# Sixteen block sums re-dealt between the token loop and the spatial mixing of layer one (seven and nine in place of six and ten)

## The chip, the core and the metric

The program runs on one core of one Trainium2 chip. The metric is the device time of one execution in microseconds (us): the median of three runs before the change is 1368.55 us, the runs lie between 1368.22 and 1369.3 us. Times inside the program are given in us from the start of the span of one profiled execution.

## The reference, cut to what is computed

Two layers follow each other, each a block A and a block B, all in float32, over a sequence of 2048 tokens of width 512. Both layers use the same weights.

```
x = x + A(layernorm(x)); x = x + B(layernorm(x))        # twice
A: qkv = x @ wqkv; linear attention of 32 heads of 16 (phi = elu + 1); @ wo
B: z = gelu(x @ w_in)                  # 2048 x 1792
   z1, z2 = halves of z; z2 = layernorm(z2)
   g = w_sp @ z2 + b_sp                # w_sp is 2048 x 2048: mixes tokens
   out = (z1 * g) @ w_out
```

The product `w_sp @ z2` is the spatial mixing. The change touches its preparation in layer one (L = 0 in the code).

## The kernel before

**Arithmetic.** Every operand of a matmul is split in two fp32r parts: a high part, rounded by ScalarE (ACT; `high`, L135, or L1457 and L1462 in the mixing), and a low part, the rest, subtracted by VectorE (DVE; `low`, L138, or L1466, L1470 and L1472). A product is then three matmuls: high by high, high by low, low by high. So TensorE (PE) is fed by a chain of load, high part, low part.

**Phases of one layer.** `P1` is the first half of A (projections and the state of the linear attention). `P2` is the loop over 16 blocks of 128 tokens that finishes A and makes z1 and z2; it runs steps s = 1 to 18 and is called the second half here. `P4` is the mixing with the output product behind it. In layer one its steps g = 0 to 47 are six products of eight steps each, in the order P4 (g 0 to 7), P1 (8 to 15), P6 (16 to 23), P7 (24 to 31), P5 (32 to 39), P3 (40 to 47), and then 14 steps of a nested product N2.

**Why there are sums.** The mixing is a 2 x 2 block product by Winograd's scheme: seven products in place of eight, of which some need sums of blocks of `w_sp` as an operand. `Sums` (L1174) makes them. One unit of it (`fetch`, `sum`, `store`) loads three 128 x 512 pieces of `w_sp` over the queue of SyncE (SP; L1195), makes three additions on GpSimd (POOL; L1209) and stores three pieces to DRAM as S1, S3 and S2 (L1202). There are 16 such units, in fixed order; number 2k + j belongs to step k of the products P6 (reads S2), P7 (S3) and P5 (S1). Sixteen more units follow, one addition and one store each, for S4 (product P3). They load a piece of S2 and one of `w_sp` (L131).

**What sets the order.** The program is recorded in the order of the Python code, and each engine and queue works through its own instructions in that order. Tables at the head of the file say at which step a unit is made:
- `TOKEN_TICKS` (L29): steps of the second half at which a unit is made. The first of its three pieces goes to the z tile of the same number, the two others to pages; the load is issued at the end of the step before. SP stores the result at the start of the next step.
- `MIX_TICKS` (L31): steps g of the mixing at which the remaining units are made, in `tick` (L1212): the load at step g - 1, the additions at step g and the stores behind them, issued by POOL.
- `MIX_UNITS` (L32): steps g at which a unit of the kept sums of N2 is made (`Inner.unit`, L1287): one addition on DVE (L1296 to L1306), a high part on ACT (L135) into a fresh page, and at the next step the low part on DVE (`finish`, L138). SP stores both (L1267). The loads of a unit (L1263) are issued two steps ahead of it.

**A step of the mixing.** `P4.run` (L1759) does for step g: `prepare(g + 2, g + 3)`, that is ACT L1457 and DVE L1466 for the weight of step g + 2, and DVE L1433, ACT L1462, DVE L1470 for the z operand of step g + 3; then the matmuls of step g (`acc`, L1619 to L1621); `fetch(g + 4)`, a load of S2 or S3 by SP (L1415), or of `w_sp` (L1413); `tick`; the unit of N2; and behind the last step of a product `evac` (L1649), in which DVE reads the six accumulating banks out (L1669 behind P6). P6 and P7 add to the same banks, so P7 can't begin in a bank that DVE has not read.

**Pages.** SBUF is dealt in 23 pages of 128 x 512 by `Slots` (L39): a page that was given back first is handed out first, and the new writer waits for the last reader or the last transfer of the page. A page behind a store is given back with a lag of six pages (`STORE`).

Of the kernel before, what the change touches and what calls it, by code (L numbers as in the profile page):

```python
# [25 lines left out]
PHI_EPS = 1e-6  # L26
DEFER = 6
STORE, POOL = 6, 3
TOKEN_TICKS = {at: (at,) for at in (5, 7, 9, 11, 12, 13)}  # L29
SPARE_TAGS = {14: 15, 16: 15}  # L30
MIX_TICKS = (2, 4, 5, 7, 8, 10, 12, 14, 16, 17, 20, 21, 23, 24, 26, 27, 29, 30, 32, 34, 35, 37, 38, 39, 40, 41)  # L31
MIX_UNITS = (10, 14, 20, 22, 25, 31, 36, 40), (1, 3, 5, 7, 9, 11, 13, 15)  # L32
MAKE_AT = 5, 7, 9
ROW_UNITS = range(1, 9)
INNER_UNITS = range(47, 55, 2)
# [55 lines left out]
def mixer_kernel(ctx: ExitStack, tc: tile.TileContext, x_in, wqkv, wo_d, win1_d, win2_d, wsp_d, bsp_d, wout_d,  # L91
# [680 lines left out]
    class P2:  # L772
# [308 lines left out]
        def run(self, sums):  # L1081
# [3 lines left out]
            for s in range(1, NT + 3):  # L1085
# [54 lines left out]
                if self.L == 0:  # L1140
                    sums.sum(s, TOKEN_TICKS)
                if s >= 15:
# [25 lines left out]
                self.xturn.load(s - 1)  # L1168
                if self.L == 0 and s + 1 in TOKEN_TICKS:
                    sums.fetch(TOKEN_TICKS[s + 1])  # L1170
            self.win2.free()
# [191 lines left out]
    class P4:  # L1363
# [395 lines left out]
        def run(self, nxt):  # L1759
# [3 lines left out]
            n = len(self.steps)  # L1763
            own, units = inner["N2" if self.nest_late else "N1"], MIX_UNITS[self.L]
            sums_at = {}
# [7 lines left out]
            for g in range(n):  # L1773
# [8 lines left out]
                if self.nest_late:  # L1782
                    self.sums.tick(g, MIX_TICKS)
                    if g == 34:
# [134 lines left out]
```

## Time and profile before

| | us |
|---|---|
| median of three runs | 1368.55 |
| the profiled execution's own time | 1368.05 |
| its span, first to last instruction | 1366.3 |
| PE busy in the span | 1354.5 |
| DVE, ACT, POOL busy | 1037.8, 638.4, 500.9 |
| PE idle in front of a matmul, all waits that the trace lists | 8.2 |
| second half of layer one, s = 1 to 18 | about 140 to 330 |
| mixing of layer one, g = 0 to 47 | 344.75 to 580 |

PE is busy almost throughout, so its few idle places, and the places where it runs slowly, are what the other engines can still give or take. A row of the timeline has the start, the duration, the engine, the line, what is written from what, how many instructions are merged in the row, and in brackets how long the engine sat idle before it and what released it. "pg" is a page, "qd" a tile of 128 x 2048, "bank" a bank of PSUM, "s" one of the sums in DRAM.

### The profile page before, as it was taken

Reading aid. Unit: us, or ns where it says so; the run is one execution under the profiler, and the core shown is the slowest. Engines: PE = TensorE matmul, PEld = TensorE weight load, DVE = VectorE, ACT = ScalarE, POOL = GpSimd, SP = SyncE. Lnnn points to the kernel's source line nnn. Section 1 sums busy time; section 2 is a strip of 40 time slices with the busy share of each in tenths; the row PEclk is TensorE's granted clock in tenths of the full one; section 3 lists DMA queues with packets and bytes.
Section 4 is the critical chain, followed back from the end, with each engine's and each line's share of the span. In section 5 each row is a group of like instructions: output and inputs, shape, how many; then the busy total and the mean of one; then the engine's idle time right before and its main releaser. Section 6 shows DMA issues by size and latency. Waiting matters only on the chain.

```text
span 1366.3 us, 18345 instructions
## 1 busy us (share of the span) xinstructions
PE 1354.5 (99%) x6087; PEld 1133.1 (83%) x6087; DVE 1037.8 (76%) x1582; ACT 638.4 (47%) x1021; POOL 500.9 (37%) x597
## 2 busy tenths in 40 slices
PE   9999999999999899999999999999999999999998
PEld 7888888888888688888888888888888888888887
DVE  7985898876867789976678768887767798978642
ACT  6875553446442333442456655444455534533310
POOL 2333475533377347426421133543230011412240
PEclk9999999999999999999999999999999999999999
DMA  5762388966798888895776534666568799569552
GB/s 182 240 210 88 123 262 257 301 229 196 240 340 302 282 275 279 267 375 185 225 254 194 197 95 122 202 210 204 187 200 280 222 339 322 187 202 317 215 183 91
DMA packets 181552, 310.18 MB, mean 227 GB/s; under 512 B 15696, under 2 KB 67920, under 8 KB 177360
## 3 DMA queue, kind: packets, MB, share of 16 engines
q1 hardware_dynamic: 166112, 250.66, 56.8%
q0 software_dynamic: 11744, 51.91, 10.5%
q10 hardware_dynamic: 3600, 6.42, 1.3%
q8 instruction: 48, 0.79, 0.2%
q14 instruction: 48, 0.39, 0.1%
HBM read 211.68 MB, written 97.26 MB: 226 GB/s over the span
## 4 chain that ended last, share of the span: by engine, by line
PE 87%; DVE 4%; DMA 3%; ACT 2%; POOL 2%; issue 1%; SPq 0%; DVEq 0%; POOLq 0%; ACTq 0%
PE bank L151 16%; PE bank L149 16%; PE bank L150 16%; PE bank L1619 8%; PE bank L1620 8%; PE bank L1621 8%; PE bank L1552 4%; PE bank L1553 4%; PE bank L1550 4%; PE bank L995 1%; PE bank L994 1%; PE bank L993 1%; DMA s<-pg 1%; POOL pg L1209 1%; DMA pg<-in_wsp_dram 1%
## 5 line engine op out<-in xcount | busy, mean ns | idle before, releaser
L1619 PE MATMUL bank<-qd,pg 128*128 128x512 f32 x544 | 212.2, 390 | 4.8 <-DVE bg L1669 4.8
L1620 PE MATMUL bank<-qd,pg 128*128 128x512 f32 x544 | 212.3, 390 | 0.0
L1621 PE MATMUL bank<-qd,pg 128*128 128x512 f32 x544 | 212.3, 390 | 0.0
L1466 DVE TENSOR_TENSOR qd<-qd,qd 128x1024 fp32r<-128x1024 f32 x104 | 144.4, 1389 | 68.9 <-ACT qd L1457 68.6
L1457 ACT ACTIVATE qd<-qd 128x1024 fp32r<-128x1024 f32 x104 | 110.1, 1059 | 140.2 <-DVE qd L1466 43.3
L151 PE MATMUL bank<-qd,pg 128*128 128x512 f32 x380 | 148.6, 391 | 0.3 <-DVE pg L138 0.3
L135 ACT ACTIVATE pg<-pg 128x512 fp32r<-128x512 f32 (+1 forms) x146 | 89.3, 620 | 118.5 <-DVE pg L330 44.3
L268 POOL TENSOR_SCALAR rs<-mv 128x1 f32<-128x1 f32 x95 | 42.1, 444 | 267.5 <-DVE mv L266 257.9
L1641 POOL TENSOR_TENSOR bg<-bg,pg 128x512 f32<-128x512 f32 x56 | 92.0, 1653 | 107.6 <-DMA pg<-z 97.7
L1619 PEld LDWEIGHTS bank<-qd,pg 128*128 128x128 f32 x544 | 102.5, 189 | 26.5 <-ACT qd L1457 5.2
L138 DVE TENSOR_TENSOR pg<-pg,pg 128x512 fp32r<-128x512 f32 (+1 forms) x143 | 110.6, 774 | 15.0 <-ACT pg L135 13.8
L1209 POOL TENSOR_TENSOR pg<-pg,pg 128x512 f32<-128x512 f32 x52 | 85.2, 1639 | 100.2 <-DMA pg<-in_wsp_dram 80.4
L1620 PEld LDWEIGHTS bank<-qd,pg 128*128 128x128 f32 x544 | 102.4, 188 | 21.4
L1621 PEld LDWEIGHTS bank<-qd,pg 128*128 128x128 f32 x544 | 102.6, 189 | 21.2
L149 PE MATMUL bank<-qd,pg 128*128 128x512 f32 x284 | 110.9, 391 | 0.4 <-ACT pg L135 0.4
L150 PE MATMUL bank<-qd,pg 128*128 128x512 f32 x284 | 110.6, 389 | 0.0
L330 DVE STREAM_TRANSPOSE pg<-pg 128x512 f32<-128x512 f32 x79 | 86.1, 1090 | 10.7 <-DMA pg<-yt 8.5
L149 PE MATMUL bank<-bg,qd 128*128 128x448 f32 x256 | 94.0, 367 | 0.0
L150 PE MATMUL bank<-bg,qd 128*128 128x448 f32 x256 | 93.7, 366 | 0.0
L151 PE MATMUL bank<-bg,qd 128*128 128x448 f32 x256 | 93.4, 365 | 0.0
L1552 PE MATMUL bank<-qd,pg 128*128 128x512 f32 x224 | 87.4, 390 | 0.3 <-DVE qd L1466 0.3
L1553 PE MATMUL bank<-qd,pg 128*128 128x512 f32 x224 | 87.2, 389 | 0.0
(221 smaller groups left out, 3217.6 us busy)
## 6 DMA issues: line engine op xcount, KB each, us to landing
qd<-s SPq DMA_DIRECT2D x64, 512.0 KB, 4.3
qd<-n POOLq DMA_DIRECT2D x32, 1024.0 KB, 7.5
pg<-in_wsp_dram SPq DMA_DIRECT2D x93, 256.0 KB, 4.8
qd<-in_wsp_dram SPq DMA_DIRECT2D x40, 512.0 KB, 4.5
pg<-z SPq DMA_DIRECT2D x56, 256.0 KB, 4.0
n<-pg SPq DMA_DIRECT2D x55, 256.0 KB, 4.4
x<-pg SPq DMA_DIRECT2D x48, 256.0 KB, 2.7
pg<-x SPq DMA_DIRECT2D x48, 256.0 KB, 3.5
```

The costliest lines, as they stand in the source:

```text
L138: nc.vector.tensor_sub(l, src, h.bitcast(F32))
L149: nc.tensor.matmul(out, ah, bh, start=start, stop=False)
L150: nc.tensor.matmul(out, ah, bl, start=False, stop=False)
L151: nc.tensor.matmul(out, al, bh, start=False, stop=stop)
L1209: nc.gpsimd.tensor_tensor(t, a, b, op=OP.add)
L1457: nc.scalar.activation(wh, r, AF.Copy)
L1466: nc.vector.tensor_sub(wl, r, wh.bitcast(F32))
L1552: m(out[i], h[:, o, f], w[:, o, 1], start=False, stop=False, skip_group_check=True)
L1553: m(out[i], l[:, o, f], w[:, o, 0], start=False, stop=last and name in ("P2", "P3", "P4"), skip_group_check=True)
L1619: m(out, h[:, o], w[:, 0, j, :], start=start, stop=False, skip_group_check=True)
L1620: m(out, h[:, o], w[:, 1, j, :], start=False, stop=False, skip_group_check=True)
L1621: m(out, l[:, o], w[:, 0, j, :], start=False, stop=stop, skip_group_check=True)
```

## The change

```diff
-TOKEN_TICKS = {at: (at,) for at in (5, 7, 9, 11, 12, 13)}
+TOKEN_TICKS = {at: (at,) for at in (5, 7, 8, 9, 11, 12, 13)}
 SPARE_TAGS = {14: 15, 16: 15}
-MIX_TICKS = (2, 4, 5, 7, 8, 10, 12, 14, 16, 17, 20, 21, 23, 24, 26, 27, 29, 30, 32, 34, 35, 37, 38, 39, 40, 41)
-MIX_UNITS = (10, 14, 20, 22, 25, 31, 36, 40), (1, 3, 5, 7, 9, 11, 13, 15)
+MIX_TICKS = (2, 4, 5, 7, 8, 10, 11, 13, 15, 20, 21, 23, 24, 26, 27, 29, 30, 32, 34, 35, 37, 38, 39, 40, 41)
+MIX_UNITS = (12, 16, 19, 22, 25, 31, 36, 40), (1, 3, 5, 7, 9, 11, 13, 15)
```

The entries of `MIX_TICKS` from 20 on are the same. Seven of the 16 threefold units are now made in the second half (steps 5, 7, 8, 9, 11, 12, 13) and nine in the mixing (2, 4, 5, 7, 8, 10, 11, 13, 15); the last is made at step 15 and was made at step 17. Three kept sums of N2 go from steps 10, 14 and 20 to 12, 16 and 19. No instruction is added or removed on any engine, and the pages are dealt out anew from the second half on.

In the rows below a name is a tile with its slot and a running number: `pg6_485` is slot 6, handed out as the 485th page.

POOL in step 8 of the second half, before: the layer norm of x (L268 to L273), the product for the denominators (L793), and the layer norm of z (L268 to L273).

```order
L268 TENSOR_SCALAR rs_2433<-mv_2431 128x1
L269 TENSOR_TENSOR rs_2433<-rs_2433,mhalf_74 128x1
L273 TENSOR_SCALAR nb_2436<-mv_2431,rs_2433 128x1
L793 TENSOR_TENSOR pg21_276_2449<-z11_q0_1525,pg20_191_1518 128x512
L268 TENSOR_SCALAR rs_2488<-mv_2486 128x1
L269 TENSOR_TENSOR rs_2488<-rs_2488,mhalf_74 128x1
L273 TENSOR_SCALAR nb_2491<-mv_2486,rs_2488 128x1
```

The same place with the change:

```order
L268 TENSOR_SCALAR rs_2439<-mv_2437 128x1
L269 TENSOR_TENSOR rs_2439<-rs_2439,mhalf_74 128x1
L273 TENSOR_SCALAR nb_2442<-mv_2437,rs_2439 128x1
L793 TENSOR_TENSOR pg14_278_2455<-z11_q0_1525,pg20_191_1518 128x512
L1209 TENSOR_TENSOR pg16_270_2400<-z8_sum_2398,pg16_270_2400 128x512
L1209 TENSOR_TENSOR z8_sum_2398<-z8_sum_2398,pg13_271_2402 128x512
L1209 TENSOR_TENSOR pg13_271_2402<-pg16_270_2400,pg13_271_2402 128x512
L268 TENSOR_SCALAR rs_2497<-mv_2495 128x1
```

Three additions now stand between L793 and the layer norm of z.

SP in steps 16 to 19 of the mixing, before. `s2_4` to `s2_7` are the pieces of S2 that the last four steps of P6 read; L1195 loads the unit made at step 17, L131 that of step 20.

```order
L1415 DMA qd1_62_4637<-s2_4_137 128x1024
L1195 DMA pg21_475_4639<-in_wsp_dram 128x512
L1195 DMA pg10_476_4641<-in_wsp_dram 128x512
L1195 DMA pg4_477_4643<-in_wsp_dram 128x512
L1267 DMA n2_8_3_163<-pg14_466_4561 128x512
L1267 DMA n2_8_3_163<-pg13_472_4602 128x512
L1415 DMA qd5_64_4678<-s2_5_138 128x1024
L1415 DMA qd4_66_4711<-s2_6_139 128x1024
L1415 DMA qd0_68_4738<-s2_7_140 128x1024
L131 DMA pg3_484_4740<-s2_0_133 128x512
L131 DMA pg6_485_4742<-in_wsp_dram 128x512
```

The same place with the change, from step 14 on, where the unit of step 15 is loaded:

```order
L1195 DMA pg10_468_4570<-in_wsp_dram 128x512
L1195 DMA pg2_469_4572<-in_wsp_dram 128x512
L1263 DMA pg5_470_4574<-in_wsp_dram 128x512
L1267 DMA n2_8_1_161<-pg4_461_4492 128x512
L1267 DMA n2_8_1_161<-pg3_464_4533 128x512
L1415 DMA qd3_60_4609<-s2_3_136 128x1024
L1415 DMA qd1_62_4650<-s2_4_137 128x1024
L1415 DMA qd5_64_4680<-s2_5_138 128x1024
L1415 DMA qd4_66_4709<-s2_6_139 128x1024
L1267 DMA n2_8_3_163<-pg16_475_4653 128x512
L1267 DMA n2_8_3_163<-pg14_478_4682 128x512
L1415 DMA qd0_68_4738<-s2_7_140 128x1024
```

The last load for a threefold unit (L1195) now stands five loads of P6 ahead of the read of `s2_7`, where it stood three ahead. The loads of the unit of step 20 (L131, into `pg1_483` and `pg10_484` with the change) stand right behind the read of `s2_7` in both.

ACT in steps 22 and 23, before: the weight and the z operand of `prepare`, the high part of the kept sum of step 22 (L135), and the next weight and z operand.

```order
L1457 ACTIVATE qd0_73_4815<-qd2_70_4769 128x1024
L1462 ACTIVATE pg7_497_4819<-pg22_496_4817 128x384
L135 ACTIVATE pg6_501_4851<-pg11_490_4777 128x512
L1457 ACTIVATE qd2_75_4853<-qd3_72_4809 128x1024
L1462 ACTIVATE pg22_503_4857<-pg3_502_4855 128x384
```

With the change:

```order
L1457 ACTIVATE qd0_73_4817<-qd2_70_4772 128x1024
L1462 ACTIVATE pg13_496_4821<-pg21_495_4819 128x384
L135 ACTIVATE pg10_500_4851<-pg15_490_4780 128x512
L1457 ACTIVATE qd2_75_4853<-qd3_72_4811 128x1024
L1462 ACTIVATE pg21_502_4857<-pg1_501_4855 128x384
```

Nothing moved here but the slot. L135 writes slot 6 before, the page (`pg6_485`) in which the sum of step 20 was made and from which it was stored; with the change it writes slot 10, and that page (`pg10_484`) again held the sum of step 20.

## The prediction

> **What bounds the kernel now.** I read the page first: how much of the span PE fills, and what it waits for.
>
> ```profile
> span 1366.3 us, 18345 instructions
> PE 1354.5 (99%) x6087; PEld 1133.1 (83%) x6087; DVE 1037.8 (76%) x1582; ACT 638.4 (47%) x1021; POOL 500.9 (37%) x597
> L1619 PE MATMUL bank<-qd,pg 128*128 128x512 f32 x544 | 212.2, 390 | 4.8 <-DVE bg L1669 4.8
> ```
>
> PE is busy for 99% of the span. The change takes no matmul away, so it can gain only where PE idles or runs slowly. The list of PE's waits, longest first, has one that is worth naming behind the start of the program.
>
> ```profile
> PE bank L1619 <- DVE bg L1669: 4.8, 1, 4.8
> PE bank L512 <- DVE pg L507: 2.0, 1, 2.0
> PE bank L149 <- ACT pg L135: 0.4, 2, 0.2
> ```
>
> One wait of 4.8 us: a matmul of the mixing waits for the read-out behind product P6. The timeline of PE shows the place, from the start of step 23 (460.35) over its last matmul to the first matmuls of step 24.
>
> ```profile
> 460.35 0.39 PE L1619 MATMUL bank<-qd,pg 128*128 128x512 f32 x1
> ...
> 464.20 0.39 PE L1621 MATMUL bank<-qd,pg 128*128 128x512 f32 x1
> 469.38 0.53 PE L1619 MATMUL bank<-qd,pg 128*128 128x512 f32 x1 [4.79 <-DVE bg L1669]
> 469.70 0.63 PE L1620 MATMUL bank<-qd,pg 128*128 128x512 f32 x1
> ...
> 473.09 0.39 PE L1619 MATMUL bank<-qd,pg 128*128 128x512 f32 x1
> ```
>
> From 460.35 to 464.20 are 17 matmuls at 0.2265 us each. PE would have gone on at 464.43; it went on at 469.38, 4.95 us later. The next nine matmuls took 3.71 us (469.38 to 473.09) and would have taken 2.04 at the old pace: another 1.67. The table by stretches says why: the granted clock.
>
> ```profile
> 460.30:464.20 3.90, 3.90 (x18) 3.20 (x18) 1.65 (x3) 0.00 (x0) 0.72 (x2) 1.00 0.97 326
> 469.40:473.10 3.70, 3.70 (x10) 2.89 (x11) 3.70 (x7) 0.33 (x1) 1.83 (x2) 0.54 0.86 260
> ```
>
> The third column from the end is the clock: 1.00 ahead of the wait, 0.54 behind it. So the whole price of this place is 4.95 + 1.67 = 6.62 us. By the idle row alone it would be 4.95 and the forecast 1.7 us higher. The Trainium skill, TensorE: Matmul & The Clock Gate (Part 1: The HAM clock gate), says that the array falls to half its clock after an idle window of about 3.4 us and needs as long under load to recover; the trace agrees, with 0.54 for 3.7 us behind 4.95 us of idle. By that rule a remaining wait well under 3.4 us costs itself and no more.
>
> Then the chain that ended last, followed back from 469.38.
>
> ```profile
> 442.54 2.16 POOL pg L1209
> 444.70 1.03 POOL s L1202 x2
> 445.73 3.45 DMA s<-pg
> ...
> 449.30 0.32 SPq L1415
> ...
> 449.67 0.42 SPq L131
> ...
> 450.21 5.18 DMA pg<-in_wsp_dram
> ...
> 455.56 1.60 POOL pg L1209
> ...
> 457.45 6.99 DMA s<-pg
> ...
> 465.14 1.05 ACT qd L1457
> ...
> 468.55 0.69 DVE bg L1669
> ```
>
> Read forward: the last threefold sum (step 17) ends on POOL at 444.70; its piece of S2 lands at 449.18. SP has stood in front of that transfer, because its next load (L1415) reads this very piece. Only then does SP issue the loads of the sum of step 20; they land at 455.4, POOL adds, and the store holds the page until 464.44. ACT wants this page for a kept sum:
>
> ```profile
> 458.21 0.53 ACT L1462 ACTIVATE pg<-pg 128x384 fp32r<-128x384 f32 x1 [0.40 <-DVE pg L1433]
> 464.60 0.63 ACT L135 ACTIVATE pg<-pg 128x512 fp32r<-128x512 f32 x1 [5.86 <-DMA s<-pg]
> ```
>
> ACT stood 5.86 us. Behind its L135 is queued L1457, on it waits DVE's L1466, and behind that stand L1470, L138 and the read-out L1669, on which PE waits.
>
> **The change, part by part.** First the last sum, at step 15. Step 19 begins four steps of 18 matmuls ahead of 460.35, at 444.04; step 16 at 431.8; step 14, two steps of 24 matmuls earlier, at 420.9. How long a unit takes from load to POOL is read from the last unit but one, loaded in step 15 (PE from 426.4).
>
> ```profile
> 426.96 1.33 SPq L1195 DMA_DIRECT2D pg<-in_wsp_dram  x3
> 432.90 5.10 POOL L1209 TENSOR_TENSOR pg<-pg,pg 128x512 f32<-128x512 f32 x3 [2.66 <-DVE bg L1666]
> 437.94 1.62 POOL L1202 DMA_DIRECT2D s<-pg  x3
> ...
> DMA to landing us min/median/max: 2.8/5.9/8.0
> ```
>
> SP issues 0.6 us into the step, POOL starts 5.9 later, adds for 5.1, issues for 1.6, and a store of a sum lands 2.8 to 8.0 us behind its issue. With the loads in step 14: 421.5, 427.4, 432.5, 434.1, and landed by 442.1 at the latest. SP comes to the read of this piece in step 19, at 444.3 (in the trace it issues a quarter of a microsecond behind a step's start, as the tile of the step before comes free). So SP's wait goes, with 2 us to spare.
>
> What is late next? The loads of the sum of step 20 still stand behind that read, and ACT's L135 in step 22 still writes the page of that sum. The head of the chain moves from 449.30 to 444.27, by 5.03 us. With every duration of the old chain kept, PE's first matmul of P7 could go at 469.38 - 5.03 = 464.35, and PE comes there at 464.43: no wait, by a hair. The largest of these durations, the store of 6.99, is above the median of 5.9, so 1.1 us more is likely to be spare. Bounds: with a store of 8.0 the wait is 0.9; if moreover DVE's L1470 runs beside POOL (1.65 us in one row, 0.55 in another) it is 2.0.
>
> ```profile
> 455.45 0.55 DVE L1470 TENSOR_TENSOR pg<-pg,pg 128x384 fp32r<-128x384 f32 x1
> 459.23 1.65 DVE L1470 TENSOR_TENSOR pg<-pg,pg 128x384 fp32r<-128x384 f32 x1
> ...
> 502.07 3.66 DVE L1673 TENSOR_TENSOR bg<-pg,bank 128x512 f32<-128x512 f32 x6
> ```
>
> The row of 502.07 is the like place eight steps later: there the read-out starts 1.6 us before product P7 ends (503.7). I take no wait, a gain of 6.6 us, between 4.6 and 6.6.
>
> Then the threefold sums at 10, 11 and 13. They stand earlier than at 10, 12, 14 and 16; two in neighbouring steps stood at 16 and 17 before, with no wait of PE there. Cost nothing; cover is the weight's lead on PE:
>
> ```profile
> 454.31 1.23 DVE L1466 TENSOR_TENSOR qd<-qd,qd 128x1024 fp32r<-128x1024 f32 x1 [3.10 <-ACT qd L1457]
> ```
>
> This low part, ready at 455.54, is that of step 23, which starts at 460.35: 4.8 us ahead, in the tightest stretch. An addition beside POOL is longer by 1.1 (L1470 above); more than four such in one step would be needed to use up the lead.
>
> The kept sums at 12, 16 and 19 are the same three instructions a unit, and their loads and stores (L1263, L1267) on SP two steps later or one earlier. The page of the unit of step 12 was stored from by the sum of step 10; by the durations above (loads in step 9, 393.7; adds to 405.3; first of three stores landed by 413.3) ACT could stand up to 3 us there. Cost nothing while the lead above holds.
>
> The extra sum in step 8 of the second half brings three loads on SP, three additions on POOL and three stores on SP at the start of step 9. The first row is of step 7, where there is such a sum already; the next three are of step 8, and PE's is the first matmul that reads DVE's L138 of 214.62.
>
> ```profile
> 202.81 2.61 DVE L913 TENSOR_TENSOR z_z<-z_z 128x384 f32<-128x384 f32 x2 [0.53 <-ACT z_z L279]
> ...
> 213.84 1.29 POOL L793 TENSOR_TENSOR pg<-z_q,pg 128x512 f32<-128x512 f32 x1
> ...
> 214.62 1.07 DVE L138 TENSOR_TENSOR qd<-pg,qd 128x512 fp32r<-128x512 f32 x1 [0.70 <-ACT qd L135]
> 216.35 0.56 DVE L913 TENSOR_TENSOR z_z<-z_z 128x384 f32<-128x384 f32 x1 [0.67 <-ACT z_z L279]
> ...
> 221.01 0.36 PE L149 MATMUL bank<-bg,qd 128*128 128x448 f32 x1
> ...
> 223.27 0.38 SPq L131 DMA_DIRECT2D pg<-qt  x1
> 226.93 0.38 SPq L315 DMA_DIRECT2D qt<-pg  x1
> ```
>
> The sum would run from 215.1 to 220.2 behind L793. DVE's L913 takes 0.56 alone and 1.3 beside a sum (2.61 for two), so DVE falls behind by a microsecond or two, at worst by the whole 5.1. PE reads the result of 215.69 at 221.01: 5.3 us of cover a step. Cost nothing, with 5.1 against 5.3 at worst. SP's three stores, 0.4 each, go into the 3.3 us between its rows of 223.27 and 226.93, behind a sum that is done by then; the three loads at the end of step 7 push the loads of x and q by 1.3 us (L1195 above), and those are read a step later.
>
> **The sum.** 1368.05 (the profiled execution's own time) - 6.6 = 1361.4. The median of the runs stands 0.5 above that execution, so 1361.9 us. Below that I see only the scatter of the runs (1368.22 to 1369.3).
>
> **The rivals.** One: a wait of 1 to 2 us remains in front of P7 (slow store, POOL beside DVE): 1362.8 to 1363.9 at the plain wait, up to 1365.6 if the slow clock's 1.67 came with it. For it: the chain fits by 0.1 us with its old durations. Against it: the 6.99 is above the median, and the stores of two sums that ran at 438 to 449 are gone from that stretch. Chance 0.18.
>
> Two: the change doesn't do what it says. The page of the sum of step 20 is again the one that the kept sum of step 22 writes, and something other than the read of S2 holds SP until 449, a page not free for the loads of step 14 or 19. Then PE waits as before: 1368.5. Against it: the page for the latter (slot 10) was last stored from by the unit made at step 15, landed by 442. Chance 0.10.
>
> Three: slower, by contention in the second half. With the new table sums stand in steps 7, 8 and 9, one behind the other. If POOL's additions stop DVE altogether, three of them cost 15.3 us, the cover gives 5.3, PE idles 10, and the slow clock adds 1.7: 11.7 - 6.6 gives 1368.5 + 5.1 = 1373.6. PE is touched from a lag of 5.3 us on; the gain of 6.6 is used up at 10.2, and the result is slower by 0.2% at 12.9. Against it: the two rows of L913, 1.3 against 0.56, and three sums in steps 11, 12 and 13 before, without a wait of PE. The Trainium skill, GPSIMD Engine Reference (1. Specifications), speaks for it: POOL shares its SBUF interfaces with DVE, in conflict with DVE instructions of two SBUF inputs. The trace agrees in kind (1.65 against 0.55), but shows no standstill. Chance 0.08.
>
> **How the numbers follow.** The forecast has 0.64, the rivals 0.18, 0.10 and 0.08. About 0.2% (2.7 us) is what a measurement of this kernel can tell from no change: the first two cases are faster (0.82), the third is the same (0.10), the last slower (0.08). The range goes from 1361.0, the scatter below the forecast, over the first rival to 1365.5; outside are the last two, 0.18.
>
> **What would show it.** In the profile with the change PE's list of waits has no L1619 behind L1669 of over a microsecond, and no stretch of clock 0.54 at 460 to 475; SP issues the read of the last piece of S2 at about 444; POOL starts the sum of step 20 at about 450, and ACT's L135 of step 22 at about 458. In the second half L1209 has three additions at about 215 and PE no new wait. I am wrong if PE idles at another place of layer one: then the step that called the cover enough has failed.

## The result and the profile after

The kernel with the change takes 1361.86 us (median, runs from 1361.23 to 1362.26), the kernel before 1368.46 us in the same series. The ratio is 0.9948, with a 95% interval from 0.9935 to 0.9961 (here and below it is worked out from all runs, so it is not exactly that of the medians). The forecast was 1361.9 us. One execution of the kernel before in a later series, of 4718.34 us, is left out of the ratios as slow.

The profiled execution of the changed kernel took 1361.72 us. From its page, the span, the engines' busy times and the group of matmuls that had waited 4.8 us before:

```profile
span 1360.0 us, 18353 instructions
PE 1353.4 (100%) x6087; PEld 1133.3 (83%) x6087; DVE 1034.1 (76%) x1582; ACT 638.1 (47%) x1021; POOL 496.3 (36%) x594
L1619 PE MATMUL bank<-qd,pg 128*128 128x512 f32 x544 | 211.9, 390 | 0.0
```

PE's busy time fell by 1.1 us only (1354.5 before; the slow matmuls are gone), the span by 6.3. What went is idle time: L1619 has 0.0 where it had 4.8. POOL has 594 instructions where it had 597: the three stores of the sum that moved to the second half are issued by SP now. So instructions do change engine, though the text ahead of the prediction says that none is added or removed on any. The list of PE's waits, longest first, now starts with one that was there before:

```profile
PE bank L512 <- DVE pg L507: 2.0, 1, 2.0
PE bank L151 <- DVE pg L138: 0.4, 2, 0.2
PE bank L1552 <- DVE qd L1466: 0.3, 1, 0.3
```

PE at the seam of P6 and P7, with the change: three matmuls a fast spacing apart, of which that of 464.57 is the first of P7.

```profile
464.35 0.39 PE L1621 MATMUL bank<-qd,pg 128*128 128x512 f32 x1
464.57 0.39 PE L1619 MATMUL bank<-qd,pg 128*128 128x512 f32 x1
464.80 0.39 PE L1620 MATMUL bank<-qd,pg 128*128 128x512 f32 x1
```

The same stretch of 469.4 to 473.1 in the table by stretches has the full clock (third column from the end), where it had 0.54:

```profile
469.40:473.10 3.70, 3.70 (x18) 3.08 (x17) 2.47 (x4) 1.02 (x3) 0.14 (x1) 1.00 0.92 300
```

And the chain, station by station, from the timeline with the change: SP's read of the last piece of S2 and the loads of the sum of step 20; POOL's addition and its store; ACT's high part of the kept sum of step 22; DVE's low parts and the read-out.

```profile
444.37 0.32 SPq L1415 DMA_DIRECT2D qd<-s  x1
444.74 0.42 SPq L131 DMA_DIRECT2D pg<-s  x1
445.27 0.36 SPq L131 DMA_DIRECT2D pg<-in_wsp_dram  x1
...
449.63 2.26 POOL L1209 TENSOR_TENSOR pg<-pg,pg 128x512 f32<-128x512 f32 x1 [15.53 <-DMA pg<-in_wsp_dram]
...
452.19 0.56 POOL L1202 DMA_DIRECT2D s<-pg  x1 [0.30 <-POOL pg L1209]
...
457.80 0.63 ACT L135 ACTIVATE pg<-pg 128x512 fp32r<-128x512 f32 x1 [4.05 <-DMA s<-pg]
458.41 1.06 ACT L1457 ACTIVATE qd<-qd 128x1024 fp32r<-128x1024 f32 x1
...
460.64 0.55 DVE L1470 TENSOR_TENSOR pg<-pg,pg 128x384 fp32r<-128x384 f32 x1
...
461.71 3.75 DVE L1669 TENSOR_TENSOR bg<-bank,pg 128x512 f32<-128x512 f32 x6
```

L135 begins 6.80 us earlier than before (464.60). Of this, 4.93 is SP's head (449.30 to 444.37); 0.33 is the way from the read to the store's issue (8.15 us before, 7.82 now); 1.54 is the store (7.15 us from its issue to L135 before, 5.61 now). From L135 to the read-out it takes 3.9 us in both. ACT still stands 4.05 us for the page, but the read-out now starts 2.86 us ahead of PE. Before, PE went on 0.83 us behind the start of the read-out (468.55 to 469.38), so some 2.0 us are to spare.

### The profile page after: what moved, and what is told of

Its sections match the earlier page's. It is cut to its first block, busy times and chain, and to the rows that moved or that the text cites. A ratio compares the mean times of both kernels' runs of the same rounds, so it can differ in the third digit from the quotient of the medians.

```text
span 1360.0 us, 18353 instructions
## 1 busy us (share of the span) xinstructions
PE 1353.4 (100%) x6087; PEld 1133.3 (83%) x6087; DVE 1034.1 (76%) x1582; ACT 638.1 (47%) x1021; POOL 496.3 (36%) x594
## 4 chain that ended last, share of the span: by engine, by line
PE 95%; DVE 3%; ACT 1%; issue 0%; POOL 0%; DVEq 0%; ACTq 0%; POOLq 0%
PE bank L151 17%; PE bank L149 17%; PE bank L150 17%; PE bank L1620 9%; PE bank L1619 9%; PE bank L1621 9%; PE bank L1552 4%; PE bank L1550 4%; PE bank L1553 4%; PE bank L995 1%; PE bank L994 1%; PE bank L993 1%; PE bank L736 1%; PE bank L512 0%; DVE pg L138 0%
## 5 line engine op out<-in xcount | busy, mean ns | idle before, releaser
L1620 PE MATMUL bank<-qd,pg 128*128 128x512 f32 x544 | 211.9, 390 | 0.0
L1619 PE MATMUL bank<-qd,pg 128*128 128x512 f32 x544 | 211.9, 390 | 0.0
L1466 DVE TENSOR_TENSOR qd<-qd,qd 128x1024 fp32r<-128x1024 f32 x104 | 140.4, 1350 | 65.2 <-ACT qd L1457 64.9
L1457 ACT ACTIVATE qd<-qd 128x1024 fp32r<-128x1024 f32 x104 | 110.1, 1059 | 132.0 <-DMA qd<-s 39.3
L135 ACT ACTIVATE pg<-pg 128x512 fp32r<-128x512 f32 (+1 forms) x146 | 89.4, 620 | 125.0 <-DVE pg L330 46.3
L268 POOL TENSOR_SCALAR rs<-mv 128x1 f32<-128x1 f32 x95 | 42.2, 444 | 260.3 <-DVE mv L266 250.7
L1620 PEld LDWEIGHTS bank<-qd,pg 128*128 128x128 f32 x544 | 102.2, 188 | 21.2
L1619 PEld LDWEIGHTS bank<-qd,pg 128*128 128x128 f32 x544 | 102.2, 188 | 21.2
L138 DVE TENSOR_TENSOR pg<-pg,pg 128x512 fp32r<-128x512 f32 (+1 forms) x143 | 106.0, 742 | 16.3 <-ACT pg L135 12.9
L1209 POOL TENSOR_TENSOR pg<-pg,pg 128x512 f32<-128x512 f32 x50 | 80.2, 1604 | 101.9 <-DMA pg<-in_wsp_dram 68.7
```

Of the source, the lines that this page charges most:

```text
L138: nc.vector.tensor_sub(l, src, h.bitcast(F32))
L1457: nc.scalar.activation(wh, r, AF.Copy)
L1466: nc.vector.tensor_sub(wl, r, wh.bitcast(F32))
L1619: m(out, h[:, o], w[:, 0, j, :], start=start, stop=False, skip_group_check=True)
L1620: m(out, h[:, o], w[:, 1, j, :], start=False, stop=False, skip_group_check=True)
```

## The experiments

In all of them the kept sum of step 22 writes the page of the sum of step 20, as before and after the change, unless said otherwise. "Idle" is PE's time without a matmul at a seam: the bracket in the row of the first matmul behind it plus 0.16 us, which is how 4.79 became 4.95 in the prediction. "Slow clock adds" is how much later the twelfth matmul behind the wait starts than at 0.2265 us apiece. Ratios are to the kernel before on the same chip, and the kernels were measured on several: sums alone, kept sums alone, last at 17 and other page beside a median of 1369.35 us; ten in the mixing, last at 16 and at 18 and nine in the second half beside 1369.27; the change again, the two variants of the kept sums and loads first beside 1367.96.

| kernel | SP's read of the last S2 piece | read-out L1669 starts | idle ahead of P7 | slow clock adds | profiled execution | median of runs, ratio |
|---|---|---|---|---|---|---|
| before | 449.30 | 468.55 | 4.95 | 1.67 | 1368.05 | |
| the change | 444.37 | 461.71 | 0 | 0 | 1361.72 | 1361.86, 0.9948 |
| sums alone | 446.00 | 463.38 | 0 (1.48 ahead of P6) | 0.10 | 1363.15 | 1365.62, 0.9975 |
| kept sums alone | 450.86 | 470.72 | 6.50 | 1.60 | 1370.40 | 1369.69, 1.0009 |
| ten in the mixing | 444.56 | 462.31 | 0 | 0 | 1361.70 | 1361.72, 0.9942 |
| last at 16 | 445.33 | 462.74 | 0 | 0 | 1361.28 | 1362.01, 0.9946 |
| last at 17 | 447.60 | 465.78 | 1.91 | 0.08 | 1363.55 | 1364.20, 0.9971 |
| last at 18 | 450.93 | 470.68 | 6.94 | 1.83 | 1370.92 | 1370.14, 1.0007 |
| other page | 448.92 | 465.43 | 1.64 | 0.12 | 1362.97 | 1365.64, 0.9973 |
| loads first | 451.07 | 466.69 | 2.83 | 1.70 | 1366.83 | 1366.54, 0.9991 |

Idle and slow clock taken off, the profiled executions lie between 1361.2 and 1362.3 us: what tells the kernels of this table apart is PE's idle time at one seam and the clock behind it, and little else. A profile shows one execution. With "sums alone" and "other page" it is the fastest of ten and of nine, 2.5 and 2.7 us below the median, so their waits in the table are likely shorter than in most of their executions; no other execution was profiled.

### The two halves of the change

The sums as in the change, the kept sums left at 10, 14 and 20:

```diff
-MIX_UNITS = (12, 16, 19, 22, 25, 31, 36, 40), (1, 3, 5, 7, 9, 11, 13, 15)
+MIX_UNITS = (10, 14, 20, 22, 25, 31, 36, 40), (1, 3, 5, 7, 9, 11, 13, 15)
```

> The block sums as in the change (seven in the second half, nine in the mixing, the last at step 15); the three kept sums stay at steps 10, 14 and 20 as before. The page of the kept sum of step 22 is again that of the sum of step 20. Theory (SP stands behind the last piece of S2, and everything on the way to the read-out is late by as much): 1361.9 us, 1361 to 1363; SP's read of the last piece at about 444.4; no wait of L1619 behind L1669 over 1 us. Rival (the kept sum that left step 20 unloaded ACT and DVE): 1368.5 us, the wait of about 4.8 us stays.

Measured: 1365.62 us, ratio 0.9975 (0.9966 to 0.9985), above the forecast range. The wait ahead of P7 is gone, as expected, but there is a new one, a product earlier. PE's waits, and from the timeline ACT's high part of the kept sum of step 14 and DVE's read-out of P1:

```profile
PE bank L1619 <- DVE bg L1666: 1.3, 1, 1.3
```

```profile
426.52 0.63 ACT L135 ACTIVATE pg<-pg 128x512 fp32r<-128x512 f32 x1 [8.21 <-PE bank L1620]
...
432.65 3.66 DVE L1666 TENSOR_TENSOR bg<-pg,bank 128x512 f32<-128x512 f32 x6
```

With the new sums the page dealt to this kept sum is one that held the high part of step 14's z operand (the releaser L1620 multiplies by it), and PE reads that to the end of step 14. ACT stands 8.21 us; the weight, and behind it DVE's read-out of P1 (L1666, 432.65), are late. With the change as it is, the read-out starts at 428.74:

```profile
428.74 4.09 DVE L1666 TENSOR_TENSOR bg<-pg,bank 128x512 f32<-128x512 f32 x6
```

The other half, the kept sums at 12, 16 and 19 and the block sums as before:

```diff
-MIX_UNITS = (10, 14, 20, 22, 25, 31, 36, 40), (1, 3, 5, 7, 9, 11, 13, 15)
+MIX_UNITS = (12, 16, 19, 22, 25, 31, 36, 40), (1, 3, 5, 7, 9, 11, 13, 15)
```

> The block sums as before (six and ten, the last at step 17); only the three kept sums go to steps 12, 16 and 19. Theory: SP's read stays at about 449.3, the wait of L1619 behind L1669 stays at 4 to 5.5 us, 1367.5 to 1369 us. Rival (the move of the kept sums is what helps): 1361.9 us and no wait.

```profile
PE bank L1619 <- DVE bg L1669: 6.3, 1, 6.3
```

1369.69 us, ratio 1.0009 (0.9997 to 1.0021): moving the kept sums alone takes nothing away. The wait is longer than the 4 to 5.5 us that were expected: SP's read comes at 450.86, 1.6 us later than before, and so does PE's product P7.

Which of the three kept sums matters, with the change itself once more beside two variants. The change again:

> The change once more, unaltered, as the measure for the three others on the same chip. Expected 1361 to 1363 us, no wait of L1619 over 1 us, PE's idle time between products P6 and P7 none.

It took 1361.84 us, ratio 0.9961 (0.9946 to 0.9976), no idle time at P7. Its profiled execution has one small wait that the first did not have, 0.8 us at 541.8 behind DVE's L1678. And here ACT's L135 of step 22, at 456.56, waits for DVE's addition (L1306) and no longer for the store: with the change the store is no longer always what comes last, and the read-out, at 461.92, is again early.

Of the kept sums only that of step 14 moved:

```diff
-MIX_UNITS = (12, 16, 19, 22, 25, 31, 36, 40), (1, 3, 5, 7, 9, 11, 13, 15)
+MIX_UNITS = (10, 16, 20, 22, 25, 31, 36, 40), (1, 3, 5, 7, 9, 11, 13, 15)
```

> The block sums of the change; of the three kept sums only that of step 14 goes to 16, the others stay at 10 and 20. With all three left in place PE had waited 1.3 us for L1666, behind an ACT L135 that stood 8.2 us for a page which the matmuls of step 14 still read. Theory (the page dealt to the kept sum of step 14 is the whole reason): no wait for L1666, 1361.9 us (1361 to 1363). Rival (the kept sums of step 10 or 20 matter): the wait of 1.3 us stays, 1363.2 us or above.

Measured 1361.99 us, ratio 0.9961 (0.9946 to 0.9976): the whole gain, with no wait for L1666. And the reverse:

```diff
-MIX_UNITS = (12, 16, 19, 22, 25, 31, 36, 40), (1, 3, 5, 7, 9, 11, 13, 15)
+MIX_UNITS = (12, 14, 19, 22, 25, 31, 36, 40), (1, 3, 5, 7, 9, 11, 13, 15)
```

> The block sums of the change; the kept sums at 12, 14 and 19: the one of step 14 alone stays in place, and its page is again one that the matmuls of step 14 read last. Theory: ACT's L135 stands until about 426.5, PE waits about 1.3 to 1.7 us for L1666 behind product P1, 1363 to 1364 us. Rival: no wait, 1361.9 us.

Measured 1365.95 us, ratio 0.9991 (0.998 to 1.0002). ACT, PE's wait, and the stretch behind it:

```profile
426.54 0.63 ACT L135 ACTIVATE pg<-pg 128x512 fp32r<-128x512 f32 x1 [7.36 <-PE bank L1620]
```

```profile
PE bank L1619 <- DVE bg L1666: 2.4, 1, 2.4
```

```profile
434.60:438.30 3.70, 3.70 (x10) 2.94 (x11) 3.70 (x6) 0.00 (x0) 0.75 (x2) 0.59 0.97 380
```

The place is as expected, the price is not: 2.60 us of idle time and another 1.69 by the clock, which has a mean of 0.59 of full speed in this stretch. So the step from 14 to 16 keeps some 4 us that the new sums would have lost; the other two kept sums are worth nothing that shows.

### Where the last sum stands

The same change with its last threefold sum at 16, 17 and 18 in place of 15 (the entry in bold of 2, 4, 5, 7, 8, 10, 11, 13, **15**). At 16:

> The change with its last sum at step 16. By the old durations the additions run at 432.9 to 438, the store of S2 is issued by 439.6 and lands 2.8 to 8.0 us later, at 442.4 to 447.6. Theory: SP's read at 444.4 to 447.6, PE waits 0 to 3 us in front of P7, 1361.9 to 1365 us, likeliest 1362.5. Rival (the gain needs the whole step from 17 to 15): over 1366 us.

1362.01 us, ratio 0.9946 (0.993 to 0.9961). The read comes at 445.33, and the read-out 1.8 us ahead of PE: one step of the two would have done.

At 17, where it stood before:

> The change, with its last threefold sum at step 17 in place of 15 (mixing 2, 4, 5, 7, 8, 10, 11, 13, 17; seven in the second half; kept sums at 12, 16, 19). Theory: the last piece of S2 lands at 447.5 to 449.2, SP's read stands until then, PE waits 3 to 5 us in front of P7, 1365.5 to 1368.5 us. Rival (what helped is that fewer additions of POOL run beside P6 at 427 to 445, or the sum in the second half): 1361.9 us.

1364.20 us, ratio 0.9971 (0.996 to 0.9982), under the expected 1365.5, but not the 1361.9 of the rival. PE's waits, SP's read, and the stretch behind the seam:

```profile
PE bank L1619 <- DVE bg L1669: 1.8, 1, 1.8
```

```profile
447.60 0.32 SPq L1415 DMA_DIRECT2D qd<-s  x1
```

```profile
466.60:470.30 3.70, 3.69 (x16) 3.09 (x17) 3.70 (x7) 0.30 (x1) 2.82 (x4) 1.00 0.95 276
```

SP still stands, but 1.7 us less than before: no sum at step 16 precedes this one on POOL, which starts it at 438.14 in place of 439.58. The idle time is 1.91 us, and the clock stays full. So the rival has a part in it: with the last sum still at its old step, 5.2 us of the medians are gone (1369.35 to 1364.20). What counts is when the last store lands, and the change brings that forward twice: by the step, and by a POOL that is free when the step comes. At 18:

> The change with its last sum at step 18. The additions run at about 442.5 to 447.5, the store of S2 lands at about 453 to 455. Theory: SP's read stands until then, 4 to 6 us later than in the kernel before, and PE's wait in front of P7 grows by as much, to 9 to 11 us; 1372.5 to 1375 us. Rival (the wait has another cause and is of fixed size): 1368.5 us.

1370.14 us, ratio 1.0007 (0.9997 to 1.0016), with 6.94 us of idle time: in the expected direction, but 1.6 us later at SP's read than the kernel before, not 4 to 6.

```profile
PE bank L1619 <- DVE bg L1669: 6.8, 1, 6.8
```

The expectation had the additions to 447.5 and a store of 5.9 us and more; POOL ended at 447.1, and SP's read went off at 450.93, so the last store landed under 4 us behind that. Over the four places the read goes 444.37, 445.33, 447.60, 450.93 and the idle time 0, 0, 1.91, 6.94: it is SP's read that sets it, and the latest place without a wait lies between 445.33 and 447.60.

### Is the sum in the second half needed, and what would more of them cost?

Six in the second half, as before, and ten in the mixing at 2, 4, 5, 7, 8, 10, 11, 12, 13, 15:

> Six sums in the second half as before, ten in the mixing at 2, 4, 5, 7, 8, 10, 11, 12, 13 and 15; kept sums as in the change. Theory (only the place of the last sum counts): 1361.9 us, 1361 to 1363; no wait in front of P7. Rival (a sum must leave the mixing, since four sums in five steps make DVE or SP late): a new wait of PE at steps 12 to 16, 1363.5 us or more.

1361.72 us, ratio 0.9942 (0.9924 to 0.996), no wait. The sum moved to the second half neither costs nor brings anything: ten sums in the mixing fit as well, as long as the last is at 15.

Nine in steps 5 to 13 of the second half, seven in the mixing at 2, 4, 5, 7, 8, 10, 13:

> Nine sums in the second half, in the nine successive steps 5 to 13, and seven in the mixing at 2, 4, 5, 7, 8, 10 and 13; kept sums as in the change. Theory (a sum in the second half is covered): 1361.9 us, 1361 to 1363, PE without a new wait at 170 to 270. Rival (additions of POOL in successive steps slow DVE there, as the third rival of the prediction had it): 5 us or more slower, 1367 us or above, with the loss at 190 to 270.

1362.85 us, ratio 0.9952 (0.9936 to 0.9968): a microsecond over the change's median, with intervals that overlap. The profile (1364.41 us, the slowest of the four executions) has one new wait of PE, at 292.24; with it, from the timeline, DVE's transposition ahead of it:

```profile
PE bank L149 <- ACT qd L135: 1.3, 1, 1.3
```

```profile
290.44 1.08 DVE L330 STREAM_TRANSPOSE pg<-pg 128x512 f32<-128x512 f32 x1 [2.42 <-DMA pg<-yt]
```

DVE waited for a transfer there (`yt`). But what makes it late goes back to POOL. First the rows of the change, then the same with nine sums:

```profile
193.43 0.42 DVE L216 TENSOR_TENSOR pg<-pg,pg 128x256 f32<-128x256 f32 x1
196.79 0.63 DVE L138 TENSOR_TENSOR pg<-pg,pg 128x512 fp32r<-128x512 f32 x1
276.30 0.49 POOL L268 TENSOR_SCALAR rs<-mv 128x1 f32<-128x1 f32 x1 [3.24 <-DVE mv L266]
```

```profile
193.56 1.40 DVE L216 TENSOR_TENSOR pg<-pg,pg 128x256 f32<-128x256 f32 x1
197.89 1.44 DVE L138 TENSOR_TENSOR pg<-pg,pg 128x512 fp32r<-128x512 f32 x1
278.18 0.49 POOL L268 TENSOR_SCALAR rs<-mv 128x1 f32<-128x1 f32 x1 [3.25 <-DVE mv L266]
```

Beside the new sum of step 6 two instructions of DVE take 1.0 and 0.8 us longer, L216 beside an addition and L138 beside a POOL instruction that has fallen behind the additions. The lag of 1.9 us is still there at 278.18, and the load of `yt` is issued at 287.62 in place of 284.58 (the other microsecond was not traced). So the third rival's contention is real, but it is some two microseconds from this one sum and not a standstill, and the cover takes most of it: PE waits 1.3 us.

### Taking the chain apart

Two edits of the kernel before, with the last sum left at 17. In the first the pages of the sums of steps 20 and 21 are given back later, so that the kept sum of step 22 gets another page:

```diff
-                        pages.put(t, lag=STORE)
+                        pages.put(t, lag=12 if m == 4 and k == 0 else STORE)
```

> The kernel before, with one edit: the pages of the first two sums of S4 (steps 20 and 21) are given back later, so that the kept sum of step 22 writes another page than the one from which the sum of step 20 is being stored. SP still stands until about 449.2. Theory (the shared page is a link that the chain can't do without): ACT's L135 of step 22 doesn't stand for a store, the read-out is early, no wait in front of P7, 1361.9 us (1361 to 1363). Rival (SP's stand delays PE by itself, through later loads; the page is an accident): 1366 to 1368.5 us.

1365.64 us, ratio 0.9973 (0.996 to 0.9985): between theory and rival. SP reads at 448.92, as before; then ACT's weight of step 24, DVE's L1470 and the addition of the kept sum, and its high part:

```profile
448.92 0.32 SPq L1415 DMA_DIRECT2D qd<-s  x1
```

```profile
456.51 1.06 ACT L1457 ACTIVATE qd<-qd 128x1024 fp32r<-128x1024 f32 x1 [2.60 <-DMA qd<-s]
...
458.75 1.65 DVE L1470 TENSOR_TENSOR pg<-pg,pg 128x384 fp32r<-128x384 f32 x1
460.32 0.68 DVE L1306 TENSOR_TENSOR pg<-pg,pg 128x512 f32<-128x512 f32 x1
...
461.11 0.63 ACT L135 ACTIVATE pg<-pg 128x512 fp32r<-128x512 f32 x1 [3.13 <-DVE pg L1306]
```

L135 no longer stands for a store, it stands for DVE. A second branch comes to light: SP's stand also delays the read of S3 for step 24 (450.31, with the change 448.49), so ACT's L1457 (456.51, with the change 452.28) and everything behind it on DVE. The issue is 1.8 us of these 4.2; the rest is the transfer, and why it took longer no run tells. By the page alone PE's idle time falls from 4.95 to 1.64 in this profile, and the clock stays full; the median, 2.7 us higher, says that other executions lose more.

In the second edit SP issues the two loads of the sum of step 20 ahead of the read at which it stands:

```diff
-                self.fetch(g + 4)
+                if g != 19:
+                    self.fetch(g + 4)
                 if self.nest_late:
                     self.sums.tick(g, MIX_TICKS)
+                if g == 19:
+                    self.fetch(g + 4)
+                if self.nest_late:
```

> The kernel before with one edit: in step 19 SP issues the two loads of the sum of step 20 (L131) ahead of its read of the last piece of S2, not behind it. The last sum stays at step 17, so SP still stands until about 449 at that read, but the sum of step 20 no longer waits for it. Theory (SP's stand works by two branches: the store of that sum and its page, and the later reads of S3 for steps 24 and 25): the first branch goes, the second stays as with the other page; POOL adds at about 450, PE waits 1 to 2 us in front of P7 at full clock, 1362.5 to 1364 us. Rival one (the loads are not what is late): 1367 to 1369 us, a wait of 4 us or more. Rival two (there is no second branch): 1361.5 us, no wait.

1366.54 us, ratio 0.9991 (0.9981 to 1.0). The timeline: loads, POOL's addition, SP's reads, ACT:

```profile
444.48 0.32 SPq L131 DMA_DIRECT2D pg<-s  x1
...
449.50 1.88 POOL L1209 TENSOR_TENSOR pg<-pg,pg 128x512 f32<-128x512 f32 x1 [3.04 <-DMA pg<-in_wsp_dram]
...
451.07 0.80 SPq L1415 DMA_DIRECT2D qd<-s  x2
...
454.76 1.06 ACT L1457 ACTIVATE qd<-qd 128x1024 fp32r<-128x1024 f32 x1 [1.64 <-DMA qd<-s]
...
457.11 1.06 ACT L1457 ACTIVATE qd<-qd 128x1024 fp32r<-128x1024 f32 x1 [0.88 <-DVE qd L1466]
...
462.01 0.63 ACT L135 ACTIVATE pg<-pg 128x512 fp32r<-128x512 f32 x1 [2.83 <-DVE pg L1306]
```

The first branch is gone here too, as expected: the sum of step 20 runs at 449.50, and ACT does not wait for its store. What is late behind SP's stand decides again, but by another way than expected: it is the piece of S2 itself (its weight, that of step 23, at 454.76), and the weight of step 24 (457.11) waits for DVE's L1466 of step 23, not for the read of S3. SP's stand lasted to 451.07, about 2 us longer than with the other page; whether the loads issued ahead of it slowed the store that it waits for, no run tells. PE's idle time is 2.83, and the table by stretches has 0.58 of the clock behind it, so it costs 4.5 us and not the 1 to 2 that were expected.

```profile
467.50:471.20 3.70, 3.69 (x10) 2.94 (x11) 3.70 (x6) 0.00 (x0) 1.27 (x1) 0.58 0.85 209
```

Taken together: with the branch over the store and its page cut, in two ways, PE still idles, so the other branch is enough for a wait; of the runs, only those in which SP's stand ends earlier have none at this seam. That the first branch alone is enough was not tested; it is read from the kernel before, where ACT stands for the store alone until 464.60. No kernel was measurably faster than the change; ten in the mixing, last at 16, and only the kept sum of step 14 moved equal it within the 0.2% that can be told apart.

## Why the prediction was right, point by point

**The price of the place, 6.62 us, all of it to be had.** Right. The two profiled executions differ by 6.33 us, and both the idle time and the slow matmuls are gone. That the median hits the forecast to 0.1 us is luck: the gain of the profiles is 0.3 us less than forecast, and the median stands 0.1 and not 0.5 us above the profiled execution. In the two later series that have a kernel of this speed, the median of the kernel before lay 6.1 and 7.6 us above it.

**SP's wait is the cause.** Right, by experiment: the place of the last sum moves SP's read, and the idle time moves with it, while the kept sums alone change nothing. The read was forecast at 444.3 and came at 444.37; POOL's start "about 450" was 449.63, ACT's L135 "about 458" was 457.80. What the prediction left out is why SP stood so long before: the sum of step 16 kept POOL busy until the last one could start, at 439.58. And for the unit made at step 15 two errors cancel: POOL began at 428.49, 1.1 us later than forecast, and added for 4.04 us, 1.1 us less than taken from the row of before.

**"By a hair."** Too cautious. The margin is some 2.0 us and not 0.08, mostly because the store took 1.54 us less than in the old chain; stores vary, and one profile does not make that a rule. The first rival (a wait that remains) did not come in the change; it is what the kernel with the last sum at 17 does.

**One chain.** Incomplete. The prediction followed the chain of waits, and that names the branch that came last. The second branch (read of S3, weight of step 24, DVE) ended only some 3 us earlier: 465.43 against 468.55 is what the other page leaves in its profile. The forecast held because both hang on SP; for an edit of the page alone the same working would have promised 6.6 and got 3.7 by the medians (1369.35 to 1365.64).

**The kept sums cost nothing.** True at the new places, but this is where the working is weakest. Steps 12 and 19 cost and bring nothing. But step 16 in place of 14 is needed, which the prediction does not see; that the change had it was luck for the forecast: at 14 the new sums lead ACT into a page that PE still reads, for 8.21 us, and PE idles 1.48 to 2.60 us behind P1. The prediction looked for cover (the weight's lead) at the new places and not at what the page order would have made of the old ones.

**The second half is covered.** Right for the change: with six, seven or nine sums there the medians lie within 1.2 us, though nine leave DVE and POOL 1.9 us behind and PE with a wait of 1.3. In the changed kernel the three new additions stand where they were put, L913 beside them takes 1.02 us (0.56 before; 1.3 were forecast), no lag is left in the next step, and no new wait of PE follows:

```profile
215.24 1.74 POOL L1209 TENSOR_TENSOR pg<-z_sum,pg 128x512 f32<-128x512 f32 x1
217.06 1.50 POOL L1209 TENSOR_TENSOR z_sum<-z_sum,pg 128x512 f32<-128x512 f32 x1
218.63 1.30 POOL L1209 TENSOR_TENSOR pg<-pg,pg 128x512 f32<-128x512 f32 x1
```

**A short wait costs itself and no more.** Wrong in its bound. Profiled idle times of 1.48, 1.64 and 1.91 us left the clock full, and the first rival's wait of 1 to 2 us would have come at its plain price by these three; 2.60 and 2.83 us were followed by 0.59 and 0.58 of it over the next 3.7 us, like 4.95 and more. The Trainium skill, TensorE: Matmul & The Clock Gate (Part 1: The HAM clock gate), has an idle window of about 3.4 us; here less than that was enough. Nor is the length of the wait shown to be all that decides. With loads first the clock fell only when PE had gone on for over half a microsecond, from 467.51:

```profile
467.50:467.80 0.30, 0.28 (x1) 0.28 (x2) 0.30 (x1) 0.00 (x0) 0.00 (x0) 1.00 1.59 184
468.10:468.40 0.30, 0.30 (x2) 0.28 (x1) 0.30 (x1) 0.00 (x0) 0.00 (x0) 0.50 0.90 348
```

Cut like this, the five slow stretches begin between 2.9 and 5.2 us behind the start of the wait. So no run here shows that a wait of 2.6 us always brings the slow clock, or that one of 1.9 us never does.

## What to carry to other kernels

Here a load that reads what a store has just written held everything behind it on SP's queue, for 8.7 us of waiting in the kernel before: look at what stands behind such a read, not only at the read. What frees it is an earlier end of the store, by an earlier place of the work or by an engine that is free for it sooner. The chain of waits names one branch, so before an edit that cuts only that branch, look for what ends next (here 3 us earlier, off the same stand); an edit at the common root eases both. And where pages are dealt in the order in which they come free, moving one piece of work deals other work a new page: look for a new writer that must wait for a long reader, as ACT's L135 in step 14.

## What the runs showed of the hardware

- The granted clock fell to 0.50 behind idle times of PE from 2.60 to 6.94 us and not behind those of 1.48 to 1.91 us, each seen in one profiled execution. It stayed there for 3.4 us (469.6 to 473.1 before) or, behind the waits of 6.50 and 6.94 us, for 6.8 us, of which PE idled half; the cost was 1.6 to 1.8 us in all five.
- Two instructions of DVE that took 0.42 and 0.63 us took 1.40 and 1.44 us beside POOL, in the kernel with nine sums in the second half.
- A store of one 128 x 512 piece that POOL issues lands after very different times: the store of the last S2 piece took 3.45 us in the chain of the kernel before and 2.81 us in that with the other page, as this chain of waits has it:

```profile
445.98 2.81 DMA s<-pg
```

- With PE's wait gone most of the scatter of the kernel's time is gone too: beside the last experiments the kernel before ran from 1362.87 to 1370.38 us, the changed one from 1361.34 to 1362.76. That the store's landing makes this scatter is likely but not shown, since one execution of each was profiled.
